# Attention kernel: chunk 0 in two query halves, reciprocals spread by TensorE from 16 columns, squares of the queries on VectorE

## The chip, the cores and the metric

The kernel runs on one core of a Trainium2 chip. The metric is the device time of one launch in microseconds (us). Most executions of one kernel agree within 0.3%; faster or slower is given at 2%. The profiled spans are 1.8 to 2.0 us shorter than the times of the same runs.

## The reference, cut to what matters

```python
x = A_x                                    # 1 x 2048 x 448, bf16
xn = _layernorm(x)
q, k, v = split(xn @ wqkv)                 # 16 heads of 28
p = softmax(q @ k.T * 28 ** -0.5)          # 16 x 2048 x 2048
s = merge(p @ v) @ wo
g = silu(gelu(xn @ w1 + b1) @ w2 + b2)     # 448 -> 1792 -> 448
return x + s * g
```

Dominant are the exponentials: 16 x 2048 x 2048 = 67 million.

## The kernel before

The Python file is a planner. Generators hand out tasks with an engine, an estimated duration and a priority; a list scheduler orders them and writes one program per engine, each strictly in order, with semaphores between them. **Whatever changes a duration or a task can change the order of everything after it.**

The work is cut into 16 blocks (4 groups of 4 heads, 4 chunks of 512 queries). A block has 64 score tiles of 128 keys x 512 queries. TensorE writes scores to a ring of PSUM banks, ScalarE takes exponentials of two (block 0) or three tiles at a time, TensorE multiplies them with v into `acc`. In some units the third tile is given to VectorE, which computes its exponential with a polynomial ("late" tiles, mostly in pairs of 1024 columns):

```python
def pick_late(self, u):            # is the third tile of unit u given to VectorE?
    ...
    left = (n - 1 - r) / 3.0 * 1.364 + LATE_SLACK      # time left in the block; LATE_SLACK = 6.0
    ...
        bl = K.backlog()                               # VectorE work that is waiting
        if not K.ys or bl > LATE_TH or bl + 4.8 > left or sub > LATE_SUB:   # LATE_TH = 8.0
            return False
```

The queries of a block are projected, squared on GpSimd, and get a norm term that TensorE sums:

```python
def p_q(self, g, c):
    ...
    yield _Task(DVE, lambda eng: eng.tensor_copy(qb, bank), [tok], [qr], 0.7, 0.0, 2)
    ...
    yield _Task(POOL, lambda eng: eng.tensor_tensor(qs, qb, qb, ALU.mult), [qr], [tq], 1.05, 0.0, 0)
    ...   # TensorE: bsel x qs, then VectorE adds it to qb
```

At a block's end the sums of the softmax become 128 x 16 reciprocals. GpSimd spreads each of the 16 columns over 32 and splits it in two bf16 parts; TensorE turns them round with an identity matrix:

```python
def p_epi(self, b):
    ...
    yield _Task(DVE, lambda eng: eng.reciprocal(K.rc[:, :], bank[:, 0:16]), ...)
    rcb = K.rc[:, :, None].to_broadcast([128, 16, 32])
    yield _Task(POOL, lambda eng: eng.tensor_copy(K.rhi[:, :, :], rcb), ...)
    yield _Task(POOL, lambda eng: eng.tensor_tensor(K.rlo[:, :, :], rcb, K.rhi[:, :, :], ALU.subtract), ...)
    ...
            for q in range(4):
                for k, r in enumerate((K.rhi, K.rlo)):
                    ap = r[:, 4 * q:4 * q + 4, :].rearrange("p a b -> p (a b)")
                    ins = eng.matmul(bank2[:, 128 * q:128 * (q + 1)], ap, K.ident[:, :], ...)
```

The dummy matmuls of zeros that appear in the trace (output `acc`, inputs `ident` and `zero`) are put in where the planner finds TensorE's recent use low, so that its clock stays up.

The softmax here doesn't subtract the row's maximum and nothing guards it: scores larger than these inputs give would overflow.

Of the kernel before, what the change touches and what calls it, by code (L numbers as in the profile page):

```python
# [16 lines left out]
DH = 28  # L17
# [27 lines left out]
for _m in sorted(MLATE):  # L45
    UOF[_m] = UOF[_m - 1]
LATE_GAP, LATE_TH, LATE_SLACK, LATE_SUB = 3, 8.0, 6.0, 14
NU = len(UNITS)
# [4 lines left out]
KNORM = 2.5  # L53
PV_START = 8
HAM_WIN, HAM_LOW, DUM = 3.4, 0.85, 0.17
# [37 lines left out]
class _Kernel:  # L93
# [167 lines left out]
    def alloc(self):  # L261
# [35 lines left out]
        self.rc = sb("rc", [128, 16], f32)  # L297
        self.rhi = sb("rhi", [128, 16, 32], bf)
        self.rlo = sb("rlo", [128, 16, 32], bf)
        self.zero = sb("zero", [128, 128], bf)  # L300
# [41 lines left out]
        self.b_x0h, self.b_vpad0 = [B(), B()], B()  # L342
        self.b_x0 = [B(), B()]
        self.b_kT = [[B() for _ in range(C)] for _ in range(G)]
        self.b_qT = [[B() for _ in range(C)] for _ in range(G)]
# [130 lines left out]
    def constants(self):  # L476
# [18 lines left out]
        def late_pads():  # L495
            yield ("until", lambda: K.b_xnT[0][1].tw is not None)

            def f(eng):
                eng.memset(K.wv[64:128, 3, :], 0.0)
                eng.memset(K.wv[0:64, 3, D:WS], 0.0)  # L500
                return eng.memset(K.wv[:, 0:3, D:WS], 0.0)
            yield _Task(DVE, f, [], [K.b_wvpad], 0.4, 0.05, 1)
            yield ("until", lambda: K.ln_done == 2 * C)
            yield _Task(DVE, lambda eng: eng.memset(K.w1[64:128, 3, :], 0.0), [], [K.b_w1pad], 0.8, 0.05, 4)
            K.dma(SP, lambda eng: eng.dma_start(K.w1[64:65, 3, :], K.B_b1.rearrange("(o f) -> o f", o=1)), K.s_b1,
                  writes=[K.b_w1pad], land=K.now + 4)
# [45 lines left out]
        def vpads():  # L552
            yield ("until", lambda: K.ready(K.b_xn[0], -0.1))
            yield _Task(POOL, lambda eng: eng.memset(K.vaug[:, :, :, DH:DH + 1], 2.0), K.b_xn[0], [K.b_vpad0], 1.2, 0.05, 2)
            yield _Task(POOL, lambda eng: eng.memset(K.vaug[:, :, :, DH + 1:32], 0.0), [K.b_vpad0], [K.b_vpad], 1.2, 0.05, 2)
# [4 lines left out]
    def loads(self):  # L560
# [11 lines left out]
        def lw(n0, n1, sem, tok, land):  # L572
            for k in range(KT):
                rows = slice(128 * k, min(128 * k + 128, D))
                ld(sv[0:rows.stop - rows.start, k, :, n0:n1], wqk[rows, :, n0:n1], sem, [tok] if k == KT - 1 else [], land)
        lw(0, 4 * DH, K.s_w["wqk"], K.b_stg, 6.5)
        ld(K.x_sb[:, 1, :, :], xr[1], K.s_x[1], [K.b_x[1]], 8.0)
# [28 lines left out]
    def p_ln(self, c):  # L606
# [5 lines left out]
        for h, ts in enumerate(hs):  # L612
            for t in ts:
                i = 4 * c + t
                yield _Task(DVE, lambda eng, i=i, t=t: eng.bn_stats(K.st6[:, i, :], K.x_sb[:, c, t, :]),  # L615
                            [K.b_x0[h] if c == 0 else K.b_x[c]], [K.b_st[c][h]], 0.61, 0.05, prio)

            def f(eng, ts=ts):
                ins = None
                for i in range(4 * c + ts[0], 4 * c + ts[-1] + 1):  # L620
                    ins = eng.bn_aggr(K.mv[:, i, :], K.st6[:, i, :])
                return ins
            yield _Task(DVE, f, [K.b_st[c][h]], [K.b_mv[c][h]], 0.1 * len(ts), 0.05, prio)
            K.spawn(K.p_ln2(c, h, ts), c)

    def p_ln2(self, c, h, ts):
# [11 lines left out]
        for t in ts:  # L638
            i = 4 * c + t
            rd = [K.b_x0[h] if c == 0 else K.b_x[c], K.b_mv[c][h], K.b_rs[c][h], K.b_pads]  # L640
            if c == 0:
                yield _Task(DVE, lambda eng, i=i, t=t: eng.tensor_scalar(
# [50 lines left out]

    def relayout(self, E, which, g0, g1, dur):
        K = self
        src = K.stg[:, :, which, 4 * g0:4 * g1, :]
        dst = (K.wq, K.wk)[which][:, :, 128 * g0:128 * g1].rearrange("p k (h e) -> p k h e", e=32)[:, :, :, 0:DH]
        if E == ACT:
# [15 lines left out]
    def p_first(self):  # L714
# [3 lines left out]
        def weights():  # L718
            yield ("until", lambda: K.b_rs[0][1].tw is not None)
            yield K.relayout(ACT, 0, 0, 1, 0.56)  # L720
            yield K.relayout(ACT, 1, 0, 1, 0.56)
            yield K.wsquare(ACT, 0, 1, 0.56)
            K.stg_done += 1
# [21 lines left out]
        def tr(pr, h):  # L745
# [3 lines left out]
            def f(eng):  # L749
# [5 lines left out]
                return ins  # L755
            return _Task(PE, f, K.b_xn[0][2 * h:2 * h + 2] + [K.b_id], [tok], 0.45, 0.2, 0)

        def trev(pr):
            for h in range(2):
                bank, tok = ring(4 * h + pr)  # L760
                src = bank.bitcast(dt.bfloat16)[:, 0:512].rearrange("p (k n) -> p k n", k=2)
                dst = K.xnT[:, 2 * pr:2 * pr + 2, 256 * h:256 * h + 256]
                rd = [tok] + ([K.b_x0h[pr]] if h else [])
                wr = [K.b_xnT[0][pr] if h else K.b_x0h[pr]]
                if pr == 0:
                    yield _Task(ACT, lambda eng, dst=dst, src=src: eng.activation(dst, src, ACTF.Copy), rd, wr, 0.6, 0.0, 0)
                else:
                    yield _Task(DVE, lambda eng, dst=dst, src=src: eng.tensor_copy(dst, src), rd, wr, 0.42, 0.0, 0)
        for h in range(2):
            for pr in range(2):  # L770
                yield tr(pr, h)
                if h == 0:
                    K.spawn(trev(pr), 0)
        K.spawn(K.p_k0(), 1)
        qps, qtok = ring(0)
        for k in range(2):
            yield K.t_proj(0, 0, 0, qps, qtok, k, 0)
        yield _Task(ACT, lambda eng: eng.activation(K.qsq[:, 0, :], qps, ACTF.Square), [qtok], [K.b_qsq[0]], 0.6, 0.0, 0)

        def f(eng):  # L780
            return eng.matmul(qps, K.bsel[:, :], K.qsq[:, 0, :], start=False, stop=True, skip_group_check=True)
        yield _Task(PE, f, [K.b_qsq[0], K.b_bsel], [qtok], 0.22, 0.15, 0)
        yield _Task(DVE, lambda eng: eng.tensor_scalar(K.qT[:, 0, 0:512], qps, K.colK[:, 0:1], None, op0=ALU.add),
                    [qtok, K.b_colK], [K.b_qT[0][0]], 0.75, 0.0, 0)

# [18 lines left out]
    def p_busy(self):  # L804
# [10 lines left out]
        while K.exp_u < NU - 2:  # L815
# [3 lines left out]
            if n > 2000:  # L819
                raise RuntimeError("stuck")  # L820

    def p_k0(self):
        K = self
        bank, tok = K.ring[:, 1, :], K.b_ring[1]
        for k in range(2):
            yield K.t_proj(1, 0, 0, bank, tok, k, 1)
        yield K.t_kev(ACT, 0, 0, bank, tok, 1)

# [50 lines left out]
    def p_q(self, g, c):  # L879
# [10 lines left out]
        qs, tq = K.qsq[:, i, :], K.b_qsq[i]  # L890
        yield _Task(POOL, lambda eng: eng.tensor_tensor(qs, qb, qb, ALU.mult), [qr], [tq], 1.05, 0.0, 0)  # L891
        bank2, tok2 = yield ("bank", lambda: K.ready([tq]) and (g == 0 or K.norms_done))
# [171 lines left out]
    def p_scores(self):  # L1064
        K = self
        for u in range(NU):
# [3 lines left out]
            for k in range(4):  # L1070
                for m, b, j, pc, _, _ in ps:
# [10 lines left out]
                    fl.append(f)  # L1082
                    rd += [K.b_qT[g][c], K.b_kT[g][t // 4]]

# [15 lines left out]
    def p_exps(self):  # L1100
        K = self
        for u in range(NU):
# [5 lines left out]
            def fexp(eng, b0=b0, p0=p0, n=n):  # L1108
                return eng.activation(K.P[:, p0:p0 + n, :], K.ring[:, b0:b0 + n, :], ACTF.Exp, scale=SM_SCALE)  # L1109
            yield _Task(ACT, fexp, [K.b_ring[b0 + k] for k in range(n)], [K.b_P[p0 + k] for k in range(n)],  # L1110
                        0.0843 + 0.4267 * n, 0.08, 3)
            for m in ms:
# [46 lines left out]
    def pick_late(self, u):  # L1159
# [8 lines left out]
        if len(ms) < 3 or not K.late_on or sub == 0 or r < 4 or GU - 1 <= u <= GU + 1:  # L1168
            return False
        left = (n - 1 - r) / 3.0 * 1.364 + LATE_SLACK  # L1170
        if K.open:
# [9 lines left out]
        else:  # L1181
            bl = K.backlog()
            one = max(bl, 4.1) + 7.2 > left
            if not K.ys or bl > LATE_TH or bl + 4.8 > left or sub > LATE_SUB:
                return False
# [44 lines left out]
    def p_exp2(self, ms, i):  # L1230
# [8 lines left out]
        tv, tu, ty = K.b_ev[n], K.b_eu[n], K.b_y[i][:len(ms)]  # L1239
        d0, d1 = (0.44, 0.74) if len(ms) == 1 else (0.71, 1.27)  # L1240
        if n == 1 and tv.w is None:
            for c in range(C):
                tv.r += K.b_kT[0][c].r
                tu.r += K.b_kT[1][c].r
# [95 lines left out]
    def p_epi(self, b):  # L1340
# [8 lines left out]
        def f(eng):  # L1349
            ins = None  # L1350
            for q in range(4):
# [4 lines left out]
        K.banks.append((bank, tok))  # L1356
        rcb = K.rc[:, :, None].to_broadcast([128, 16, 32])
        En, d1, d2 = POOL, 0.62, 1.05
        yield _Task(En, lambda eng: eng.tensor_copy(K.rhi[:, :, :], rcb), [K.b_rc], [K.b_rhl], d1, 0.0, 1)  # L1359
        yield _Task(En, lambda eng: eng.tensor_tensor(K.rlo[:, :, :], rcb, K.rhi[:, :, :], ALU.subtract),  # L1360
                    [K.b_rc, K.b_rhl], [K.b_rhl], d2, 0.0, 1)
        bank2, tok2 = yield ("bank", lambda: K.ready([K.b_rhl], 0.2))

        def f(eng):
            ins = None
            for q in range(4):
                for k, r in enumerate((K.rhi, K.rlo)):
                    ap = r[:, 4 * q:4 * q + 4, :].rearrange("p a b -> p (a b)")
                    ins = eng.matmul(bank2[:, 128 * q:128 * (q + 1)], ap, K.ident[:, :], start=(k == 0), stop=(k == 1),
                                     skip_group_check=True)  # L1370
            return ins
        yield _Task(PE, f, [K.b_rhl, K.b_id], [tok2], 0.55, 0.15, 3)
        dst = K.qT[:, g, c * 512:(c + 1) * 512]
# [101 lines left out]
```

## Time and profile before

| what | before |
|---|---|
| time, median of 4 runs | 490.1 us (490.01 to 490.25) |
| profiled span, mean granted clock of TensorE | 488.5 us, 0.994 |
| first exponential of scores starts | 13.74 us |
| late tiles | 67 |
| GpSimd busy | 86.5 us |

What ScalarE waited for (columns: total us, times, longest), exponentials only:

```profile
ACT P L1109 <- PE ring L1078: 3.7, 5, 1.2
ACT P L1109 <- PE acc L1295: 0.3, 1, 0.3
```

Four microseconds of waits are listed. The view leaves out short ones, so I also counted start to start in the trace: an exponential of three tiles follows the one before it by 1.331 us at the median, one of two by 0.905; what a gap has beyond that (and beyond the 1.587 of each of four tanh instructions that lie between) I call **stall**. Before has 10.7 us of stall: 2.6 before 45 us (block 0) and 8.1 after it.

The groups by form that the change touches (busy us, mean ns of one):

```profile
L1360 POOL TENSOR_TENSOR rlo<-rc,rhi 128x512 bf16<-128x512 f32 x15 | 20.2, 1344 | 1.2
L891 POOL TENSOR_TENSOR qsq<-qT 128x512 bf16<-128x512 bf16 x15 | 23.7, 1581 | 122.6 <-DVE qT L886 100.8 <-PE acc L811 21.8
L1247 DVE SCALAR_TENSOR_TENSOR kT<-kT 128x1024 f32<-128x1024 f32 x17 | 21.3, 1254 | 0.1
```

The square averages 1,581 ns, but its fastest takes 1,039; the 124 VectorE operations of 1024 columns with two inputs (L1247 is one kind) average 1,263 ns; undisturbed they take about 1,215 (the median).

### The profile page before, as it was taken

How to read it: one execution, taken by the hardware profiler on the slowest of the kernel's cores; microseconds unless marked ns; L12 is line 12 of the kernel's file. 1: busy time of each engine (PE TensorE's matmuls, PEld its weight loads, DVE VectorE, ACT ScalarE, POOL GpSimd, SP SyncE). 2: the span in 40 equal slices, each digit the busy share in tenths (PEclk: the TensorE clock that was granted, in tenths of full speed). 3: DMA queues.
4: the chain of work that ended last, by engine and by line, in shares of the span. 5: the costliest groups of instructions: out<-in, count | busy, mean ns of one | idle time of the engine just before them, and what ended most of it. 6: DMA issues, size and time to landing. Idle time of an engine off the chain costs nothing.

```text
span 488.5 us, 9994 instructions
## 1 busy us (share of the span) xinstructions
PE 449.2 (92%) x4143; PEld 177.4 (36%) x4179; DVE 404.8 (83%) x580; ACT 470.7 (96%) x391; POOL 86.5 (18%) x91
## 2 busy tenths in 40 slices
PE   6999999998988898999999999999999999989995
PEld 4443334333332332333333343233333333433653
DVE  8744899889998999999998299998988979878454
ACT  4999999999999999999999999999999999999994
POOL 6472112023021212020101022220200102020100
PEclk9999999999999999999999999999999999999998
DMA  8401000000000000000400000000101010101010
GB/s 250 142 12 26 1 0 1 1 1 3 0 1 1 1 0 1 2 2 0 129 5 1 0 2 1 0 2 1 38 1 40 1 38 1 58 20 38 4 50 30
DMA packets 8287, 11.08 MB, mean 23 GB/s; under 512 B 1649, under 2 KB 6897, under 8 KB 8242
## 3 DMA queue, kind: packets, MB, share of 16 engines
q1 hardware_dynamic: 8098, 10.21, 6.9%
q8 instruction: 33, 0.54, 0.5%
q10 hardware_dynamic: 144, 0.23, 0.1%
q14 instruction: 12, 0.10, 0.1%
HBM read 8.61 MB, written 1.84 MB: 21 GB/s over the span
## 4 chain that ended last, share of the span: by engine, by line
PE 37%; ACT 29%; issue 18%; DVE 12%; POOL 2%; DMA 1%; ACTq 0%; DVEq 0%; POOLq 0%
ACT P L1109 24%; PE ring L1078 11%; PE acc L1295 7%; PE misc L1026 5%; PE acc L811 4%; ACT h L1005 3%; PE misc L968 3%; PE misc L680 2%; DVE x_sb L1253 2%; PE misc L1384 1%; POOL rlo L1360 1%; DVE x_sb L1132 1%; ACT w L1040 1%; DVE st L615 1%; DVE kT L1247 1%
## 5 line engine op out<-in xcount | busy, mean ns | idle before, releaser
L1109 ACT ACTIVATE P<-ring 128x1536 bf16<-128x1536 f32 (+1 forms) x350 | 430.1, 1427 | 4.8 <-PE ring L1078 3.7
L1078 PE MATMUL ring<-qT,kT 32*128 32x512 bf16 (+1 forms) x1208 | 136.5, 350 | 17.4 <-ACT P L1109 13.3
L1295 PE MATMUL acc<-P,vaug 128*32 128x512 bf16 (+1 forms) x1141 | 93.8, 351 | 2.1 <-DVE E_sb L1345 0.7
L1078 PEld LDWEIGHTS ring<-qT,kT 32*128 32x128 bf16 x1208 | 36.6, 91 | 124.8 <-ACT P L1109 109.7
L1359 POOL CAST rhi<-rc 128x512 bf16<-128x512 f32 x15 | 19.5, 1297 | 239.7 <-DVE rc L1355 198.3
L811 PE MATMUL acc<-ident,zero 128*128 128x128 bf16 x660 | 56.4, 221 | 1.1 <-POOL qsq L891 0.6
L1132 DVE TENSOR_SCALAR x_sb<-ring 128x512 int32<-128x512 f32 x67 | 45.9, 686 | 10.4 <-PE ring L1078 9.5
L1026 PE MATMUL misc<-w,h 128*128 128x448 bf16 x224 | 51.9, 355 | 0.3
L811 PEld LDWEIGHTS acc<-ident,zero 128*128 128x128 bf16 x660 | 38.6, 98 | 24.5 <-issue 20.5
L891 POOL TENSOR_TENSOR qsq<-qT 128x512 bf16<-128x512 bf16 x15 | 23.7, 1581 | 122.6 <-DVE qT L886 100.8
L1295 PEld LDWEIGHTS acc<-P,vaug 128*32 128x32 bf16 x1141 | 24.5, 94 | 49.6 <-issue 42.3
L968 PE MATMUL misc<-xnT,w 128*128 128x512 bf16 x127 | 36.7, 382 | 2.0 <-issue 1.5
L951 DVE CAST h<-misc 128x512 bf16<-128x512 f32 x35 | 24.0, 687 | 5.4 <-PE misc L968 5.2
L1026 PEld LDWEIGHTS misc<-w,h 128*128 128x128 bf16 x224 | 17.4, 97 | 24.0 <-issue 10.6
L1251 DVE SCALAR_TENSOR_TENSOR kT<-kT 128x1024 f32<-128x1024 f32 (+1 forms) x23 | 25.8, 1121 | 0.3
L1253 DVE SCALAR_TENSOR_TENSOR x_sb<-x_sb,kT 128x1024 uint16<-128x1024 int32 (+1 forms) x23 | 25.5, 1110 | 0.3
L1247 DVE SCALAR_TENSOR_TENSOR kT<-kT 128x1024 f32<-128x1024 f32 (+1 forms) x23 | 25.5, 1107 | 0.3
L1249 DVE SCALAR_TENSOR_TENSOR kT<-kT 128x1024 f32<-128x1024 f32 (+1 forms) x23 | 25.1, 1092 | 0.3
L1251 DVE SCALAR_TENSOR_TENSOR w<-w 128x1024 f32<-128x1024 f32 (+1 forms) x21 | 23.2, 1105 | 0.2
L1247 DVE SCALAR_TENSOR_TENSOR w<-w 128x1024 f32<-128x1024 f32 (+1 forms) x21 | 22.7, 1079 | 0.3
L1249 DVE SCALAR_TENSOR_TENSOR w<-w 128x1024 f32<-128x1024 f32 (+1 forms) x21 | 22.7, 1082 | 0.1
L1253 DVE SCALAR_TENSOR_TENSOR x_sb<-x_sb,w 128x1024 uint16<-128x1024 int32 (+1 forms) x21 | 22.5, 1073 | 0.2
(144 smaller groups left out, 471.3 us busy)
## 6 DMA issues: line engine op xcount, KB each, us to landing
h<-in_A_x_dram SPq DMA_DIRECT2D x4, 448.0 KB, 3.3
w<-in_B_w_dram SPq DMA_DIRECT2D x1, 1568.0 KB, 7.3
x_sb<-in_A_x_dram SPq DMA_DIRECT2D x3, 448.0 KB, 5.2
w<-in_B_w_dram SPq DMA_DIRECT2D x1, 1344.0 KB, 9.0
out_dram<-h SPq DMA_DIRECT2D x6, 224.0 KB, 1.9
h<-in_A_wqkv_dram SPq DMA_DIRECT2D x3, 168.0 KB, 5.4
out_dram<-h SPq DMA_DIRECT2D x4, 112.0 KB, 1.7
wo<-in_A_wo_dram SPq DMA_DIRECT2D x16, 24.5 KB
```

The source lines that it names most:

```text
L811: ins = eng.matmul(K.acc[:, 0:128], K.zero[:, :], K.ident[:, :], start=False, stop=True, skip_group_check=True)
L951: yield _Task(DVE, lambda eng: eng.tensor_copy(dst, bank), [tok], wr, 0.69, 0.0, 2)
L968: ins = eng.matmul(bank, K.w1[:, kt, ft * 128:(ft + 1) * 128], K.xnT[:, kt, c * 512:(c + 1) * 512], start=(kt == 0), stop=(kt == KT - 1))
L1026: ins = eng.matmul(ps, hv[:, ft, t * 128:(t + 1) * 128], K.w2[:, ft, :], start=(ft == 0), stop=(ft == FT - 1))
L1078: return eng.matmul(K.ring[:, RB[m], col:col + nq], K.kT[32 * j:32 * j + 32, g, t * 128:(t + 1) * 128], K.qT[32 * j:32 * j + 32, g, c * 51 ...
L1109: return eng.activation(K.P[:, p0:p0 + n, :], K.ring[:, b0:b0 + n, :], ACTF.Exp, scale=SM_SCALE)
L1132: yield _Task(DVE, lambda eng, m=m, i=i, half=half: eng.tensor_scalar(K.ysb[i][:, 512 * half:512 * half + 512], K.ring[:, RB[m], :], SM_SC ...
L1247: yield _Task(DVE, lambda eng: eng.scalar_tensor_tensor(u, v, EXP_A, v, op0=ALU.add, op1=ALU.mult), [tv], [tu], d1, 0.0, 4)
L1249: yield _Task(DVE, lambda eng: eng.scalar_tensor_tensor(u, u, EXP_B, u, op0=ALU.add, op1=ALU.mult), [tu], [tu], d1, 0.0, 4)
L1251: yield _Task(DVE, lambda eng: eng.scalar_tensor_tensor(u, v, EXP_D, u, op0=ALU.mult, op1=ALU.add), [tv, tu], [tu], d1, 0.0, 4)
L1253: yield _Task(DVE, lambda eng: eng.scalar_tensor_tensor(pl.bitcast(dt.uint16), y, 2.0 ** -9, u, op0=ALU.mult, op1=ALU.add), ty + [tu], [K. ...
L1295: return eng.matmul(K.acc[32 * j:32 * j + 32, q0:q0 + nq], K.vaug[:, t, 4 * g + j, :], ap[:, col:col + nq], tile_position=(0, 32 * j), sta ...
```

## The change

It has four intents: start the exponentials earlier (chunk 0's queries in two halves of 256, so that their transposes, projections and norms overlap), unload GpSimd (reciprocals as 16 columns, spread by 32 narrow matmuls; squares of the queries and half of the layer norms on VectorE), and set the lateness limits anew for each block. Core of the diff, the start cut to its essence:

```diff
-LATE_GAP, LATE_TH, LATE_SLACK, LATE_SUB = 3, 8.0, 6.0, 14
+LATE_GAP, LATE_SUB = 3, 14
+THS = (8.0, 4.0, 7.0, 6.0, 4.0, 6.0, 9.0, 6.0, 3.0, 3.0, 8.0, 8.0, 8.0, 3.0, 6.0, 8.0)
+SLACKS = (6.0, 5.0, 6.5, 5.0, 9.0, 6.5, 9.0, 6.0, 3.0, 4.0, 6.0, 6.0, 8.0, 6.0, 8.0, 6.0)
-PV_START = 8
+PV_START = 5
...
-            if c == 0:
+            if c == 0 or t % 2 == 0:          # layer norm of these rows on VectorE, the others on GpSimd
...
+    def p_q0(self, h, bank, tok):             # for each half h of chunk 0's queries
+        ps, c0 = bank[:, 0:256], 256 * h
+        yield _Task(ACT, ... eng.activation(K.qsq[:, 0, c0:c0 + 256], ps, ACTF.Square) ...)
+        yield _Task(PE, ... eng.matmul(ps, K.bsel[:, :], K.qsq[:, 0, c0:c0 + 256], ...) ...)
+        yield _Task(DVE, ... eng.tensor_scalar(K.qT[:, 0, c0:c0 + 256], ps, K.colK[:, 0:1], None, op0=ALU.add) ...)
...
-        yield _Task(POOL, lambda eng: eng.tensor_tensor(qs, qb, qb, ALU.mult), [qr], [tq], 1.05, 0.0, 0)
+        yield _Task(DVE, lambda eng: eng.tensor_tensor(qs, qb, qb, ALU.mult), [qr], [tq], 0.43, 0.0, 2)
...
-                        0.0843 + 0.4267 * n, 0.08, 3)      # planner's duration of an exponential
+                        0.0725 + 0.4267 * n, 0.08, 3)
...
-        yield _Task(En, lambda eng: eng.tensor_copy(K.rhi[:, :, :], rcb), ...)
-        yield _Task(En, lambda eng: eng.tensor_tensor(K.rlo[:, :, :], rcb, K.rhi[:, :, :], ALU.subtract), ...)
+        yield _Task(POOL, lambda eng: eng.tensor_copy(K.rhi[:, :], K.rc[:, :]), ...)
+        yield _Task(POOL, lambda eng: eng.tensor_tensor(K.rlo[:, :], K.rc[:, :], K.rhi[:, :], ALU.subtract), ...)
...
-                    ins = eng.matmul(bank2[:, 128 * q:128 * (q + 1)], ap, K.ident[:, :], ...)
+                    for j in range(4):
+                        ins = eng.matmul(bank2[32 * j:32 * j + 32, 128 * q:128 * (q + 1)],
+                                         r[:, 4 * q + j:4 * q + j + 1].to_broadcast([128, 32]), K.ident[:, :],
+                                         tile_position=(0, 32 * j), ...)
```

## The prediction

> **What bounds the kernel now.** I read the page first: busy shares, then the 40 slices.
>
> ```profile
> PE 449.2 (92%) x4143; PEld 177.4 (36%) x4179; DVE 404.8 (83%) x580; ACT 470.7 (96%) x391; POOL 86.5 (18%) x91
> ...
> ACT  4999999999999999999999999999999999999994
> ```
>
> ScalarE (ACT) is the bound: it has work in all slices but the first and the last. TensorE's 92% is padded: 56.4 us of it are 660 matmuls of zeros (row L811 of the groups) that only keep its clock up. So the time is: when the first exponential of scores starts, plus ScalarE's work, plus ScalarE's waits, plus the tail after the last exponential. Only what shortens one of these four counts.
>
> **The start**, from the timeline:
>
> ```profile
> 12.52 0.73 DVE L783 TENSOR_SCALAR qT<-ring,colK 128x512 bf16<-128x512 f32 x1
> ...
> 13.31 0.39 PE L1078 MATMUL ring<-qT,kT 32*128 32x512 bf16 x4
> ...
> 13.74 6.57 ACT L1109 ACTIVATE P<-ring 128x1024 bf16<-128x1024 f32 x7 [0.39 <-PE ring L1078]
> ```
>
> The first exponential starts at 13.74 us. Ahead of it stands a serial chain on all 512 queries of chunk 0: evacuation of the transposes, projection (10.19 to 11.31), square (11.35 to 11.95), the norm's matmul (12.04 to 12.42), eviction (12.52 to 13.25), scores.
>
> **The work.** Groups by form: 250 exponentials of three 512-column tiles, 99 of two. Start to start I measured medians of 1,331 and 905 ns in the trace. 67 of the 99 are units that gave their third tile to VectorE ("late" tiles, row L1132, x67), so one more late tile saves ScalarE 0.43 us. It costs VectorE some 3.6 us: 0.69 for the eviction, and half of 0.71 + 4 x 1.26 for a pair.
>
> **The waits.** Of ScalarE's waits between 40 and 482 us, three are long. One is in the timeline at 155, two at 437:
>
> ```profile
> 154.66 1.42 POOL L891 TENSOR_TENSOR qsq<-qT 128x512 bf16<-128x512 bf16 x1 [16.70 <-PE acc L811]
> ...
> 155.22 1.41 DVE L1253 SCALAR_TENSOR_TENSOR x_sb<-x_sb,w 128x512 uint16<-128x512 int32 x1
> ...
> 156.68 0.40 PE L1295 MATMUL acc<-P,vaug 128*32 128x512 bf16 x4 [0.57 <-DVE x_sb L1253]
> ...
> 157.88 2.37 ACT L1109 ACTIVATE P<-ring 128x1536 bf16<-128x1536 f32 x2 [0.55 <-PE ring L1078]
> ```
>
> ```profile
> 433.07 1.50 POOL L1359 CAST rhi<-rc 128x512 bf16<-128x512 f32 x1 [22.23 <-DVE rc L1355]
> ...
> 434.65 2.09 POOL L1360 TENSOR_TENSOR rlo<-rc,rhi 128x512 bf16<-128x512 f32 x1
> ...
> 436.79 0.23 PE L1369 MATMUL misc<-ident,rhi 128*128 128x128 bf16 x1 [1.65 <-POOL rlo L1360]
> ...
> 437.78 2.79 ACT L1109 ACTIVATE P<-ring 128x1536 bf16<-128x1536 f32 x2 [1.15 <-PE ring L1078]
> ...
> 441.44 2.42 ACT L1109 ACTIVATE P<-ring 128x1536 bf16<-128x1536 f32 x2 [0.87 <-PE ring L1078]
> ```
>
> The reader is to see one pattern. In the first, L1253 on 512 columns takes 1.41 us instead of its 0.69, beside GpSimd's (POOL's) square. TensorE's in-order stream waits for it, and scores queued behind come late: ScalarE idles 0.55. In the second, GpSimd's spread of the reciprocals takes 1.50 + 2.09 us where the last block's takes 0.61 + 1.05; TensorE waits 1.65 for it ahead of the next scores, and ScalarE loses 1.15. TensorE's clock then drops (granted 0.95 in 420 to 440; four L1384 matmuls take 1.70 us instead of 0.93), which costs another 0.87. Sum 2.57 us.
>
> **What the Trainium skill says.** "SBUF — State Buffer", section "Who interferes with whom": a VectorE instruction with two SBUF inputs contends with a GpSimd instruction that reads SBUF. The trace agrees: L1251 at 65.71 takes 1.64 instead of 1.22 us beside a square that takes 1.95 instead of 1.04. "TensorE: Matmul & The Clock Gate", Part 1: idleness lowers TensorE's clock; the stretch at 437 to 441 agrees. The same page, Part 3: 32-column tiles run side by side, measured 2.38 times for three. The trace agrees: 32 context matmuls of 128 columns, four abreast, take 0.63 us at 474.02. "VectorE: DVE Perf Modes", the perf-mode tier table: a 16-bit tensor_tensor in SBUF runs at two elements a cycle. The trace has 0.39 us for 448 columns (L1395); for 512 I estimate 0.42.
>
> **The change, part by part.**
>
> Start. Three pieces. (a) The weights of q are laid out in ScalarE's idle time between 6.07 and 7.17; the weights' fourth transfer is issued at 2.66 and takes 3.8, so lands near 6.5, just in time. The squares of the weights (0.58) leave ScalarE. It therefore takes the second half's transposes at about 9.1, not 9.46: xnT is complete near 9.85 instead of 10.24, saving 0.4. (b) The last half's square, norm matmul and eviction work on 256 columns. I estimate 0.37, 0.24 and 0.46 against 0.60, 0.38 and 0.73: saves 0.6. (c) Four matmuls of 256 columns replace four of 512 that ran with a norm matmul between (1.12 us, to some 0.65): saves 0.4. Against that, the first half's square, norm matmul, evictions and key projection share the queues: give back 0.3. Net 1.1: first exponential near 12.65.
>
> Reciprocals. Per block, 15 times, GpSimd's 1.30 + 1.34 us (rows L1359, L1360; 39.7 us in all) become two operations on 16 columns, near 0.2 each like L523's 0.19. TensorE's eight matmuls (0.62 at 436.79) become 32 narrow ones, four abreast: 0.63 by the comparison above. TensorE loses nothing; the wait for GpSimd shrinks by 2 to 3 us a block, which only counted at 437: 1.15 + 0.87 = 2.02 us.
>
> Squares. 15 of 1.58 us leave GpSimd (23.7), and 15 x 0.42 = 6.3 us come to VectorE. Six normalisations (0.38) go to VectorE too: 2.3. Against this, VectorE's two-input operations are no longer stretched: 124 of 1024 columns average 1.26 against 1.22 undisturbed, 5 us. VectorE is thus about 3 us worse. The wait at 157 (0.55) goes.
>
> GpSimd: 86.5 - 39.7 - 23.7 - 4.3 + 30 x 0.2 + 1 = near 26 us.
>
> Thresholds. Ten of them are lowered and a few slacks raised, VectorE's times in the planner are shortened (1.27 to 1.14). I can't derive the number of late tiles from that. VectorE idles 7.6 us in 360 to 400 and 10.5 in 420 to 460, but under 2 in most stretches of 20 us before 260. I choose three more late tiles, 70 instead of 67: 3 x 0.43 = 1.3 us.
>
> Tail: from the last exponential's end (482.2) to the end 6.3 us; unchanged.
>
> Sum: -1.1 (start) - 2.6 (waits) - 1.3 (late tiles) + 1.0 (my allowance for small waits that a re-planned order brings; the present ones near block ends are 0.2 to 0.45 each) = -4.0. **486.0 us.**
>
> **Rivals.**
>
> (1) VectorE becomes the limit. The squares queue there, lower thresholds refuse late tiles. For it: it is 90% busy before 260 us. Against: the contention goes. Five late tiles fewer cost 2.1 us, so the time would be 489.5.
>
> (2) The early start is lost at once. The keys of chunk 2 are late already:
>
> ```profile
> 28.92 0.75 DVE L691 TENSOR_SCALAR kT<-ring,ecol 128x512 bf16<-128x512 f32 x1 [2.19 <-PE ring L680]
> ...
> 30.16 6.78 ACT L1109 ACTIVATE P<-ring 128x1024 bf16<-128x1024 f32 x7 [0.75 <-PE ring L1078]
> ```
>
> An exponential that arrives 1.1 earlier waits 1.1 longer, unless the keys come earlier too. They should: with half of the normalisations on VectorE, GpSimd's 2.81 us for chunk 2 become 1.4. If they don't, 487.1.
>
> (3) Weight loads that read one column 32 times are slow. 32 one after another at the 95 ns of a load would be 3 us, in order ahead of the scores: 1 to 1.5 us of ScalarE idle per block, 15 to 22 us in all, time over 500. Nothing in this trace shows such a load; the narrow ones here (row L1295) overlap. Small chance.
>
> (4) Everything goes well and VectorE's idle time in the second half fills with eight late tiles: -1.1 - 2.6 - 3.4 = 483.
>
> **Range and chances.** From (4) and (1), trimmed: 483.2 to 488.6. Faster by over 2% means under 480.2, which needs some fourteen more late tiles on top of all else: 4%. Slower by over 2% needs (3): 2%. Within 2%: 94%.
>
> **What the changed profile would show.** First exponential at 12.4 to 12.9. The gap at 30 gone or under 0.9. No ScalarE wait over 0.5 us after 40 us, and TensorE's clock never down before the tail. GpSimd near 26 us, its two spread operations under 0.3 us each; the 32 spread matmuls within 0.7 us. VectorE's 1024-column operations at 1.21 to 1.23 on average, its busy time 405 to 425. Two-tile exponentials: 96 to 110 instead of 99. Wrong would make me: fewer late tiles, spread matmuls over 1 us, or new waits at each block's end.

## The result, and the profile after

| | before | after |
|---|---|---|
| time, median of 4 runs | 490.1 us (490.01 to 490.25) | 486.96 us (486.47 to 488.1) |
| profiled span, granted clock | 488.5, 0.994 | 484.7, 0.997 |
| first exponential | 13.74 | 12.61 |
| late tiles | 67 | 62 |
| stall in block 0 / after 45 us | 2.57 / 8.15 | 2.17 / 3.54 |
| VectorE two-input operations of 1024 columns, mean | 1,263 ns (x124) | 1,219 ns (x132) |

The ratio is 0.9939 (95%: 0.9921 to 0.9957), so "same" by the 2% rule, though the interval excludes 1. (Ratios are the mean time of one kernel's runs over that of the other's of the same rounds, so not quite the ratio of the medians quoted.) The profiled pair differs by 3.8 us of span, a little more than the medians' 3.1, because the profiled run of the changed kernel was the fastest of its four, and that of the kernel before (490.38) was above its four.

The head of the page, as it answers to the first fence of the prediction:

```profile
PE 438.8 (91%) x4393; PEld 170.2 (35%) x4428; DVE 389.7 (80%) x562; ACT 471.8 (97%) x393; POOL 34.5 (7%) x71
...
ACT  5999999999999999999999999999999999999994
```

GpSimd went from 86.5 to 34.5 us, VectorE from 404.8 to 389.7 although it took over work: it has fewer late tiles, and its operations are no longer stretched. ScalarE is still the bound in every slice. The start, from the timeline:

```profile
11.64 0.48 DVE L814 TENSOR_SCALAR qT<-ring,colK 128x256 bf16<-128x256 f32 x1
...
12.61 1.02 ACT L1136 ACTIVATE P<-ring 128x1024 bf16<-128x1024 f32 x1 [0.42 <-PE ring L1105]
```

The eviction of the second half of the queries takes 0.48 us where all 512 took 0.73, and ends at 12.12 instead of 13.25. ScalarE's waits for exponentials, and the groups that were changed:

```profile
ACT P L1136 <- PE ring L1105: 0.4, 1, 0.4
```

```profile
L1384 POOL CAST rhi<-rc 128x16 bf16<-128x16 f32 x15 | 7.8, 521 | 403.7 <-DVE rc L1382 304.4 <-PE acc L1322 73.8 <-PE ring L1105 25.5
L1385 POOL TENSOR_TENSOR rlo<-rc,rhi 128x16 bf16<-128x16 f32 x15 | 6.2, 413 | 1.2
L918 DVE TENSOR_TENSOR qsq<-qT 128x512 bf16<-128x512 bf16 x15 | 6.3, 419 | 0.4
L1274 DVE SCALAR_TENSOR_TENSOR kT<-kT 128x1024 f32<-128x1024 f32 x18 | 21.9, 1216 | 0.3
L1136 ACT ACTIVATE P<-ring 128x1024 bf16<-128x1024 f32 x94 | 101.9, 1126 | 0.7 <-PE ring L1105 0.4
```

The one wait left in the first view is that of the first exponential itself. In the second, the spread takes 521 and 413 ns on GpSimd, more than the 200 I expected; the VectorE operation L1274 is back at its undisturbed 1,216 ns; and of the 94 two-tile exponentials 32 belong to block 0, which leaves 62 late tiles. Last, the stretch from 420 to 460 us in the view by windows (columns: length, then busy us and count of PE, PEld, DVE, ACT, POOL, then clock, DMA share, GB/s), first before, then after:

```profile
420.00:460.00 40.00, 36.18 (x449) 16.74 (x447) 29.45 (x45) 37.86 (x31) 4.85 (x4) 0.96 0.09 34
```

```profile
420.00:460.00 40.00, 35.92 (x554) 17.43 (x555) 27.34 (x40) 40.00 (x32) 2.24 (x4) 1.00 0.05 19
```

ScalarE was idle for 2.1 of these 40 us and is not any more; the clock of TensorE no longer drops.

**Where the 3.8 us of span come from.** First exponential 1.13 earlier; stall in block 0 down 0.40; stall after 45 us down 4.61, of which the three long waits that the prediction shows are 3.24 counted start to start; five late tiles fewer put 5 x 0.43 = 2.13 us of exponentials back on ScalarE; tail 0.10 shorter; the rest, some 0.3, lies in the gelu stretch (0.13 longer) and the last exponentials. -1.13 - 0.40 - 4.61 + 2.13 - 0.10 + 0.3 = -3.8.

### The profile page after: what moved, and what is told of

It is laid out like the page before. It is cut to its first block, busy times and chain, and to the rows that moved or that the text cites. A ratio compares the mean times of both kernels' runs of the same rounds, so it can differ in the third digit from the quotient of the medians.

```text
span 484.7 us, 10440 instructions
## 1 busy us (share of the span) xinstructions
PE 438.8 (91%) x4393; PEld 170.2 (35%) x4428; DVE 389.7 (80%) x562; ACT 471.8 (97%) x393; POOL 34.5 (7%) x71
## 4 chain that ended last, share of the span: by engine, by line
ACT 45%; PE 34%; issue 16%; DVE 3%; POOL 0%; ACTq 0%; DVEq 0%
ACT P L1136 43%; PE ring L1105 9%; PE acc L1322 5%; PE misc L1053 5%; PE ring L995 4%; PE acc L845 2%; PE misc L683 2%; PE misc L995 1%; PE misc L1411 1%; PE acc L827 1%; ACT h L1032 1%; ACT w L1067 1%; PE ring L937 1%; PE misc L1394 0%; PE misc L1246 0%
## 5 line engine op out<-in xcount | busy, mean ns | idle before, releaser
L1322 PE MATMUL acc<-P,vaug 128*32 128x512 bf16 (+1 forms) x1146 | 94.8, 351 | 1.2 <-DVE E_sb L1372 0.5
L1159 DVE TENSOR_SCALAR x_sb<-ring 128x512 int32<-128x512 f32 x62 | 42.6, 688 | 20.8 <-PE ring L1105 20.2
L845 PE MATMUL acc<-ident,zero 128*128 128x128 bf16 x546 | 47.0, 221 | 0.6 <-DVE E_sb L1372 0.4
L1322 PEld LDWEIGHTS acc<-P,vaug 128*32 128x32 bf16 x1146 | 25.1, 94 | 49.9 <-issue 45.0
L845 PEld LDWEIGHTS acc<-ident,zero 128*128 128x128 bf16 x546 | 31.6, 98 | 20.7 <-issue 16.9
L995 PE MATMUL misc<-xnT,w 128*128 128x512 bf16 x125 | 35.2, 382 | 1.9 <-issue 1.4
L1384 POOL CAST rhi<-rc 128x16 bf16<-128x16 f32 x15 | 7.8, 521 | 403.7 <-DVE rc L1382 304.4
L1276 DVE SCALAR_TENSOR_TENSOR kT<-kT 128x1024 f32<-128x1024 f32 (+1 forms) x20 | 23.3, 1167 | 0.3
L1278 DVE SCALAR_TENSOR_TENSOR kT<-kT 128x1024 f32<-128x1024 f32 (+1 forms) x20 | 23.3, 1167 | 0.3
L1280 DVE SCALAR_TENSOR_TENSOR x_sb<-x_sb,kT 128x1024 uint16<-128x1024 int32 (+1 forms) x20 | 23.3, 1164 | 0.4
L1274 DVE SCALAR_TENSOR_TENSOR kT<-kT 128x1024 f32<-128x1024 f32 (+1 forms) x20 | 23.3, 1163 | 0.4
L995 PE MATMUL ring<-xnT,w 128*128 128x512 bf16 x81 | 19.5, 380 | 0.9 <-ACT h L1032 0.7
L1274 DVE SCALAR_TENSOR_TENSOR w<-w 128x1024 f32<-128x1024 f32 (+1 forms) x17 | 19.7, 1159 | 0.3
L1278 DVE SCALAR_TENSOR_TENSOR w<-w 128x1024 f32<-128x1024 f32 (+1 forms) x17 | 19.7, 1157 | 0.3
L1280 DVE SCALAR_TENSOR_TENSOR x_sb<-x_sb,w 128x1024 uint16<-128x1024 int32 (+1 forms) x17 | 19.7, 1156 | 0.2
L1276 DVE SCALAR_TENSOR_TENSOR w<-w 128x1024 f32<-128x1024 f32 (+1 forms) x17 | 19.6, 1154 | 0.1
```

Of the source, the lines that this page charges most:

```text
L845: ins = eng.matmul(K.acc[:, 0:128], K.zero[:, :], K.ident[:, :], start=False, stop=True, skip_group_check=True)
L995: ins = eng.matmul(bank, K.w1[:, kt, ft * 128:(ft + 1) * 128], K.xnT[:, kt, c * 512:(c + 1) * 512], start=(kt == 0), stop=(kt == KT - 1))
L1159: yield _Task(DVE, lambda eng, m=m, i=i, half=half: eng.tensor_scalar(K.ysb[i][:, 512 * half:512 * half + 512], K.ring[:, RB[m], :], SM_SC ...
L1274: yield _Task(DVE, lambda eng: eng.scalar_tensor_tensor(u, v, EXP_A, v, op0=ALU.add, op1=ALU.mult), [tv], [tu], d1, 0.0, 4)
L1276: yield _Task(DVE, lambda eng: eng.scalar_tensor_tensor(u, u, EXP_B, u, op0=ALU.add, op1=ALU.mult), [tu], [tu], d1, 0.0, 4)
L1278: yield _Task(DVE, lambda eng: eng.scalar_tensor_tensor(u, v, EXP_D, u, op0=ALU.mult, op1=ALU.add), [tv, tu], [tu], d1, 0.0, 4)
```

## The experiments

Names beginning with b are the kernel before with one part of the change; those beginning with a are the changed kernel with one part undone or altered. They ran in three batches, beside which the kernel before had medians of 490.03, 490.06 and 489.93. "Stall" is counted as above, after 45 us.

| run | median us | ratio (95%) | late | first exp. | stall after 45 us |
|---|---|---|---|---|---|
| before | 490.1 | | 67 | 13.74 | 8.15 |
| after | 486.96 | 0.9939 (0.9921-0.9957) | 62 | 12.61 | 3.54 |
| b_narrow | 487.37 | 0.9946 (0.9933-0.9958) | 67 | 13.98 | 5.01 |
| b_start | 486.82 | 0.9940 (0.9927-0.9952) | 67 | 12.81 | 5.80 |
| b_squares | 493.41 | 1.0068 (1.0055-1.0080) | 69 | 13.50 | 9.12 |
| a_noise | 491.99 | 1.0044 (1.0030-1.0058) | 62 | 13.17 | 8.02 |
| a_th4 | 489.98 | 1.0000 (0.9988-1.0011) | 54 | 12.68 | 3.21 |
| a_th9 | 490.40 | 1.0016 (1.0002-1.0030) | 71 | 12.65 | 10.66 |
| a_wide | 489.40 | 0.9983 (0.9970-0.9996) | 61 | 12.84 | 5.94 |
| a_poolsq | 488.01 | 0.9961 (0.9949-0.9974) | 61 | 12.68 | 4.04 |
| b_narrow_start | 486.73 | 0.9935 (0.9923-0.9947) | 67 | 12.97 | 4.66 |
| a_t1 | 486.93 | 0.9940 (0.9923-0.9957) | 68 | 12.54 | 5.14 |
| a_t4 | 484.76 | 0.9908 (0.9893-0.9923) | 67 | 12.84 | 3.35 |
| a_poolxn | 490.48 | 1.0028 (1.0002-1.0055) | 59 | 12.43 | 2.92 |

The first exponential of one and the same start varies by half a microsecond and more from run to run (13.50 to 13.98 with the old one, 12.43 to 13.17 with the new one), so differences of that size there mean nothing. The means are 13.74 (3 profiles) and 12.75 (11), so the new start gains about 1.0.

The runs also differ by TensorE's clock. In seven of the profiles (before, b_start, b_squares, a_noise, a_wide, a_poolsq and a_t1) the granted clock falls to half for one stretch of 3.4 us, in four of them after TensorE had idled for 0.7 to 1.7 us at a time. Before and a_noise by windows (the clock is the third number from the right):

```profile
438.14:441.56 3.42, 3.42 (x20) 1.09 (x18) 1.76 (x3) 2.55 (x3) 0.00 (x0) 0.50 0.00 0
```

```profile
108.45:111.86 3.41, 3.41 (x18) 0.62 (x18) 3.34 (x5) 2.08 (x3) 0.80 (x1) 0.50 0.00 0
```

Of the runs without a profile only the mean clock is on record. Of the 31 runs of before beside the experiments, ten have a mean of 0.996 or more and took 489.40 to 489.56 us; the others have 0.994 or less and took 489.78 to 490.59. The changed kernel's slowest run (488.1 us) has 0.994 against 0.997 to 0.999 in the other three. So some tenths of a microsecond in before, and 2 in two runs of a_t4, go with the clock of the single run. What makes it fall in one run and not in another was not tested.

### Narrow reciprocals alone, order held

```diff
-        self.rhi = sb("rhi", [128, 16, 32], bf)      # rlo likewise
+        self.rhi = sb("rhi", [128, 16], bf)
 # two GpSimd operations on 16 columns and 32 narrow matmuls as in the change,
 # but the planner keeps the old durations 0.62, 1.05 and 0.55: every engine keeps its order
```

> The kernel before with only the reciprocals changed to 16 columns and 32 narrow matmuls; the planner keeps the old durations, so that every engine has its old order. My theory (GpSimd's slow spread cost 1.15 + 0.87 us at 437 us and nothing elsewhere): 488.1 us, no ScalarE wait at 437, 67 late tiles. Rival (another wait takes its place, or narrow matmuls with repeated columns are slow): 490 us or more.

487.37 us, 2.66 less than before. As the order is the same instruction for instruction, this is the cleanest of all runs. ScalarE's waits:

```profile
ACT P L1109 <- PE ring L1078: 1.7, 3, 0.8
```

Two of the five waits are gone, those at 437 and 441 us in the prediction's fence: in the start-to-start count 1.36 and 0.98 us of stall vanish, 2.34 together. All stall after 45 us fell by 3.14, so 0.8 went elsewhere; "nothing elsewhere" in my theory was wrong. The 32 narrow matmuls took 0.62 us on TensorE (434.78 to 435.40), their weight loads 92 to 97 ns each and overlapping; so **rival 3 is dead**. The VectorE operations of 1024 columns fell from 1,263 to 1,225 ns. The gain was larger than the prediction's 2.02 for this part.

### The early start alone, old limits

```diff
+    # p_first, p_q0, the weights and their layout as in the change
 # left as before: reciprocals, squares, layer norms, LATE_TH and LATE_SLACK
```

> The kernel before with only chunk 0 in two halves (no normalisations moved to VectorE, old thresholds; planned again). My theory: first exponential near 12.6 us and 489.0 us. Rival (the keys of chunk 2 take it back): first exponential as early, but ScalarE waits 1.5 us or more for scores near 29 us, and the time is 490.0 us.

486.82 us, 3.2 less than before, and neither number I expected. The first exponential is 0.93 us earlier, and no stall appears at 28 us to take it back, although the layer norms stayed on GpSimd. The other 2 us come from elsewhere: even in its profile, stall after 265 us is 2.08 instead of 4.59. The waits at 437 and 441 are gone here as well, without any change to the reciprocals, because the planner laid out the rest differently. **A run that lets the planner re-plan tests the part and a new order together.** Only b_narrow and a_noise (and b_narrow_start against b_start) hold the order; the others are read with that in mind. And the profile of b_start fell on its slowest run (488.22 us, the other four 486.72 to 486.96): in it the clock fell to half at 44.23 us, and the 1.15 us of stall at 47.76 follow. Its stall in the table is thus too high for the other runs by about 1.3 us.

### Squares on VectorE alone, old limits

```diff
-        yield _Task(POOL, lambda eng: eng.tensor_tensor(qs, qb, qb, ALU.mult), [qr], [tq], 1.05, 0.0, 0)
+        yield _Task(DVE, lambda eng: eng.tensor_tensor(qs, qb, qb, ALU.mult), [qr], [tq], 0.43, 0.0, 2)
```

> The kernel before with only the squares of the queries on VectorE (old thresholds; planned again, 69 late tiles instead of 67). My theory (less contention, late tiles worth 0.43 us each): 490.1 - 0.55 - 0.85 = 488.7 us. Rival (without new thresholds VectorE is overbooked, so scores and context matmuls wait for it): 491 us or more, with ScalarE waits over 0.5 us at block ends.

493.41 us, 3.4 more than before. The waits:

```profile
ACT P L1109 <- PE acc L1295: 3.2, 3, 1.4
...
ACT h L1005 <- PE ring L968: 2.4, 1, 2.4
```

The kind that was 0.3 us is 3.2: at 133.45 and 135.79, at a block's end, exponentials wait for the context matmuls (L1295), which come behind VectorE's late tiles. These are waits as in rival 1, VectorE as the limit. But they are the smaller part: all stall after 45 us is only 0.97 us higher, and two more late tiles save 0.85. The gelu stretch, which stall leaves out, takes 30.65 us instead of 28.10, 2.42 of it in the one wait of the second line, at 275.96. Shortly before, TensorE had waited for GpSimd's wide spread (which ends at 269.71) and then for VectorE's L1374 (until 271.40). The order is a new one, so this run doesn't show how much of the 3.4 us the squares themselves cost.

### GpSimd's load put back as operations that nobody waits for

```diff
+    def noise(self, n):                     # on GpSimd, into a scratch buffer nobody reads
+        ... eng.tensor_tensor(self.scr, ident, ident, ALU.mult) ... # 128 x 512, bf16
 # noise(1) after each eviction of the queries, where the square was; noise(2) after rlo at each block's end
```

> The changed kernel with GpSimd's old load put back as operations that nobody waits for: one 512-column tensor_tensor beside each square, two after each spread. All other engines keep their order. Theory (waits for GpSimd in order cost, contention alone costs little): within 0.6 us of the changed kernel's 487.0, VectorE's 1024-column operations back at 1.25 us or more. Rival (contention itself is what cost): 488.5 to 489.5 us, with ScalarE waits back.

The order of all other engines is that of the changed kernel, GpSimd is busy for 91.3 us, a little more than the 86.5 before the change, and the results of its 45 added operations are not used. If the removed *wait* had been all, nothing should happen. It cost 5.0 us: 491.99, more than the rival's range too. Stall after 45 us went from 3.54 to 8.02. TensorE's listed waits for GpSimd are the same as without the added operations (1.0 and 0.7 us). One of the places, from the timeline:

```profile
103.83 2.48 POOL L1377 TENSOR_TENSOR scr<-ident 128x512 bf16<-128x512 bf16 x2
...
104.10 1.31 DVE L1277 TENSOR_SCALAR w<-x_sb 128x1024 f32<-128x1024 uint16 x1
105.45 1.94 DVE L1278 SCALAR_TENSOR_TENSOR w<-w 128x1024 f32<-128x1024 f32 x1
107.31 0.68 DVE L1414 TENSOR_TENSOR qT<-misc,E_sb 128x512 bf16<-128x512 f32 x1
...
108.05 0.68 PE L685 MATMUL misc<-xnT,wq 128*128 128x512 bf16 x2 [1.26 <-DVE qT L1414]
...
109.32 1.45 ACT L1140 ACTIVATE P<-ring 128x1536 bf16<-128x1536 f32 x1 [0.73 <-PE ring L1109]
```

The reader is to see a chain of four engines. Beside GpSimd's two scratch operations, which last until 106.31, VectorE takes 1.31 us for what takes 0.69 elsewhere, then 1.94 instead of 1.22. Its next operation, L1414, therefore ends late; TensorE, in order, waits 1.26 us for it ahead of the next scores; ScalarE waits 0.73. Nobody waits for GpSimd here. Then TensorE's clock falls to half from 108.45 to 111.86 us (the window shown above), and ScalarE stalls twice more, at 111.38 and 113.29. The three stalls come to 2.2 us, half of what the run added. All five runs have a mean clock of 0.989 to 0.994, the changed kernel's 0.994 to 0.999: a part of the price of contention is paid through the clock, it seems. VectorE's busy time rose from 389.7 to 402.4 us. My theory before this run, that the direct waits for GpSimd carry most of the gain and contention little, **fell**: contention alone, with the falls of the clock that it brings, is worth up to 5 us in this order (a bit less for the load that was really taken away, which was smaller).

### One limit for all blocks: 4 and 9

```diff
-THS = (8.0, 4.0, 7.0, 6.0, 4.0, 6.0, 9.0, 6.0, 3.0, 3.0, 8.0, 8.0, 8.0, 3.0, 6.0, 8.0)
-SLACKS = (6.0, 5.0, 6.5, 5.0, 9.0, 6.5, 9.0, 6.0, 3.0, 4.0, 6.0, 6.0, 8.0, 6.0, 8.0, 6.0)
+THS = (4.0,) * 16       # a_th4;  a_th9: (9.0,) * 16
+SLACKS = (6.0,) * 16
```

> The changed kernel with thresholds of 4 and slacks of 6: 54 late tiles instead of 62. My arithmetic: 487.0 + 8 x 0.43 = 490.4 us, stalls unchanged. Rival (fewer late tiles also take stalls away): 489 us or less, stalls after 45 us under 3 us.

> The changed kernel with thresholds of 9 and slacks of 6 in every block: 71 late tiles instead of 62, VectorE's backlog allowed to grow. My prediction's arithmetic (each late tile saves 0.43 us and costs nothing else): 487.0 - 9 x 0.43 = 483.1 us. Rival (an overbooked VectorE delays its evictions, TensorE waits in order and so does ScalarE): 487.5 us or more, ScalarE's stalls after 45 us 7 us or more instead of 3.5.

Late tiles 54 and 71, against 62. (With the old limits of 8 and 6 the planner stops with an error on the changed kernel, so some limit had to change. But it finishes with 6 and 6, 8 and 5 or 8 and 7 in all blocks, so a set block by block was not needed for that. These were only built, not run.) Fewer tiles: 489.98 us, 3.0 more than the changed kernel; 8 x 0.43 = 3.4 is what the tiles account for, and stall is about the same, 3.21. Up to here each late tile is worth its 0.43 us. More tiles: 490.40, also more by 3.4, although nine tiles should save 3.9. Stall went from 3.54 to 10.66:

```profile
ACT P L1136 <- PE acc L1322: 5.2, 4, 2.6
```

```profile
430.07 1.22 DVE L1280 SCALAR_TENSOR_TENSOR x_sb<-x_sb,kT 128x1024 uint16<-128x1024 int32 x1
...
431.75 0.60 PE L1322 MATMUL acc<-x_sb,vaug 128*32 128x512 bf16 x5
...
432.48 2.79 ACT L1136 ACTIVATE P<-ring 128x1536 bf16<-128x1536 f32 x2 [2.61 <-PE acc L1322]
```

At a block's end the last context matmuls (L1322, which read the late tiles' `x_sb`) cannot run before VectorE has finished the last late tile at 431.29, and the exponentials run out of buffers that these matmuls free: 2.61 us of ScalarE, six times what a late tile saves. So late tiles have a price on both sides, and what decides is not their number alone but where VectorE's queue stands at the end of each block.

### Wide reciprocals, and squares on GpSimd, in the changed kernel

```diff
 # a_wide: rhi, rlo, their two operations and the eight matmuls as before the change
 # a_poolsq:
-        yield _Task(DVE, lambda eng: eng.tensor_tensor(qs, qb, qb, ALU.mult), [qr], [tq], 0.43, 0.0, 2)
+        yield _Task(POOL, lambda eng: eng.tensor_tensor(qs, qb, qb, ALU.mult), [qr], [tq], 1.05, 0.0, 0)
```

> The changed kernel with the reciprocals spread by GpSimd to 512 columns again (planned again with those durations, 61 late tiles). Theory (GpSimd's long reads stretch VectorE and the spread stands in TensorE's way): 489 to 490 us, stalls after 45 us 5.5 us or more, VectorE's 1024-column operations near 1.25 us. Rival (the new plan makes room for it): 487.4 us, the one late tile's worth.

> The changed kernel with the queries' squares on GpSimd again (planned again, 61 late tiles). Theory (15 long reads of GpSimd beside VectorE's two-input operations cost ScalarE): 488.3 us or more, stalls after 45 us 4.3 us or more. Rival (only the reciprocals' contention counted): 487.4 us, the late tile's worth.

Undoing the reciprocals costs 2.4 us (489.40), of which 0.43 is one late tile fewer, and the old wait returns near the same place:

```profile
432.59 1.90 POOL L1387 TENSOR_TENSOR rlo<-rc,rhi 128x512 bf16<-128x512 f32 x1
...
435.55 2.79 ACT L1136 ACTIVATE P<-ring 128x1536 bf16<-128x1536 f32 x2 [0.96 <-PE ring L1105]
```

In three of its five runs the clock is 0.994, and in the profile 1.17 us of its stall, at 47.37, follow a fall of the clock at 44.65; the two runs at 0.996 and 0.997 took 488.65 and 488.61.

Undoing the squares costs 1.05 us (488.01), of which 0.43 is one late tile fewer; the stall of 4.04 lies, like the time, between the two expectations. So with the new limits the squares on VectorE seem to help a little, where b_squares, with the old ones, was 3.4 slower.

### Reciprocals and start together, old limits

```diff
 # b_start, and the reciprocals of b_narrow with the planner's old durations
```

> The kernel before with the start in halves and the narrow reciprocals, in the order of the run with the start alone (486.8 us): squares still on GpSimd, old thresholds, 67 late tiles. Theory (the re-planned order of that run already escaped the wait at 437 us, so the narrow reciprocals only take contention away): 485.8 us. Rival (the two gains add, -3.2 and -2.7): 484.1 us. In both cases the squares and thresholds of the change would not have been needed.

486.73 us: the gains of the two, 2.7 and 3.2, do not add up; I had expected some 0.9 less. The order of b_start had already lost the waits that narrow reciprocals take away. And it equals the changed kernel (486.96) **without** squares on VectorE, layer norms on VectorE or new limits. These three together bought nothing that can be measured in this choice of limits. Even b_start alone, with the old reciprocals, takes 486.82: the start and the order that the planner then found give, as far as can be measured, all that the whole change gives.

### All later layer norms on GpSimd again

```diff
-            if c == 0 or t % 2 == 0:
+            if c == 0:
```

> The changed kernel with the normalisations of chunks 1 to 3 on GpSimd alone again (planned again, 59 late tiles). My prediction's rival 2 (the keys of chunk 2 then come late): a ScalarE stall of 0.8 us or more near 28 us, and 487.0 + 3 x 0.43 + 0.9 = 489.2 us. Other theory (the keys are in time anyway, as in the run with the start alone): no stall there over 0.5 us, 488.3 us.

490.48 us, 3.5 more (one run of six, 494.84, had a granted clock of 0.984; the others are 489.89 to 491.8). Rival 2 had placed the danger at 28 us. Both expectations (489.2 and 488.3) are missed. There is one stall of 3.17 us, but at 22 to 26:

```profile
25.88 1.94 ACT L1136 ACTIVATE P<-ring 128x1024 bf16<-128x1024 f32 x2 [2.47 <-PE acc L1322]
```

The exponential waits for context matmuls, so for room in the P buffers, not for keys. The planner ordered the rest anew (59 late tiles), so this run doesn't show that half of the layer norms *must* be on VectorE.

### Two other sets of limits

```diff
+THS = (8.0, 7.0, 8.0, 6.0, 6.0, 7.0, 5.0, 9.0, 9.0, 9.0, 7.0, 9.0, 10.0, 7.0, 8.0, 8.0)        # a_t4
+SLACKS = (6.0, 3.0, 5.0, 8.0, 3.0, 5.5, 6.0, 6.0, 7.0, 6.0, 9.0, 10.0, 10.0, 7.0, 5.0, 6.0)
-                        0.0725 + 0.4267 * n, 0.08, 3)
+                        0.051 + 0.4267 * n, 0.08, 3)
 # a_t1: another set of THS and SLACKS, the duration left at 0.0725
```

> The changed kernel with other thresholds and slacks, block by block, for which the planner finds 68 late tiles without waits of its own making. If six more late tiles come without new stalls: 487.0 - 6 x 0.43 = 484.4 us, stalls 5.7 us. Rival (as with 71 late tiles, an overbooked VectorE gives it back): 487 us or more, stalls 8 us or more.

> As the last one, with 67 late tiles, and with the planner's cost of an exponential lowered to 1.331 us for three tiles, the start-to-start time in the traces. Without new stalls 484.9 us; rival: 487 us or more, because the plan's slack is gone.

a_t1 has 68 late tiles and 486.93 us: its six more tiles save 2.6, its stall after 45 us is 1.6 higher, and its runs spread from 485.47 to 488.25; the expectation is missed. (By spans it is some 1.1 us faster than the changed kernel, 484.0 against 485.15 at the median; four of its six times are 2.5 to 3.1 us above their spans, and why is not known.) **a_t4 is the fastest: 484.76 us**, as expected (484.9), ratio 0.9908, 5.2 less than the kernel before. By medians it is 2.2 less than the changed kernel, by the ratios 1.5, and the two intervals just touch. Two of its six runs took 486.48, with a clock of 0.991 instead of 0.997 to 0.999. It has 67 late tiles as before the change, and no more stall than the changed kernel (3.35):

```profile
PE 433.9 (90%) x4279; PEld 164.1 (34%) x4314; DVE 405.4 (84%) x587; ACT 469.5 (97%) x393; POOL 42.8 (9%) x71
```

VectorE is again as busy as before the change, 405.4 us, with the same number of late tiles, though it has squares and layer norms besides. The room for them is for the most part what the missing contention left: 124 operations that take some 1.21 us instead of 1.263 are 6 us. The rest comes from the polynomials' other operations, and from pairing: 34 pairs of late tiles and 7 single ones instead of 31 and 13. Five late tiles more than the changed kernel are 5 x 0.43 = 2.1 us, which is about the difference. Which of its two edits does it, the limits or the planner's duration of an exponential, was not tried apart.

## Why the prediction was right or wrong

486.0 was predicted, 486.96 measured, inside the range. But the sum is closer than its terms.

**Start (-1.1): right in sum, by luck in its parts.** 12.65 predicted, 12.61 measured, closer than one start repeats. Piece (a) failed. ScalarE does evacuate its last transposes early (until 9.80 us), but the last copy is VectorE's, and that ends at 10.33 us where it ended at 10.24 before:

```profile
9.83 0.41 DVE L768 COPY xnT<-ring 128x512 bf16<-128x512 bf16 x1
```

```profile
9.92 0.41 DVE L771 COPY xnT<-ring 128x512 bf16<-128x512 bf16 x1
```

So -0.4 became +0.1. From there the last projection ends after 0.51 us instead of 1.07 (0.56 saved, 0.4 predicted), the scores start 1.34 after that instead of 2.00 (0.66 saved, 0.6 predicted), and the 0.3 given back did not show. The gap at 30 us is gone. Block 0 lost 0.40 us of stall beyond that.

**Waits (-2.6, and +1.0 for new small ones): right in kind, too small.** The three long waits went, as predicted, by the mechanism that b_narrow shows with the order held: there 2.34 us of the 3.14 of stall that vanish are the two waits near 437. The clock that the prediction read as 0.95 over 20 us is half for 3.42 us, from 438.14. But all stall after 45 us fell by 4.61, where 2.6 - 1.0 = 1.6 was predicted. The allowance for new waits was wrong in sign: the small waits shrank as well. What I left out is the contention itself. I counted 5 us less of VectorE time and set them off against the squares and norms that VectorE takes over ("VectorE is thus about 3 us worse"; the sum gives 3.6), as if only the balance of busy time counted. a_noise shows that they count by where they fall: they delay operations that an in-order TensorE waits for, and put back into the same order they cost 5.0 us of time.

**Late tiles (-1.3): the step that failed.** "I choose three more late tiles, 70 instead of 67: 3 x 0.43 = 1.3 us." There were five fewer, +2.1 us: the lower limits refuse them, as the first half of rival 1 said; a_th9 and a_t1, which differ from the changed kernel in the limits alone, have 71 and 68. The price of 0.43 us held, as a_th4 shows; the number could not be had from busy shares. The direction could have been: ten limits go down, and a limit refuses tiles. (The prediction says that a few slacks are raised; six are, but four are lowered, which refuses tiles too.) I let VectorE's idle time after 360 us decide instead, but a_th9 shows that filling it costs more at the blocks' ends than it saves.

The two errors, 3.4 us for the tiles (+2.1 instead of -1.3) and 3.4 for the stalls (-5.0 in all instead of -1.6), cancel, and that the sum came so close is luck. They are not independent: a_th9 shows how stalls grow when tiles are added without regard to the blocks' ends.

**Rivals.** (1) came half true: its five fewer tiles, but not its time of 489.5, because the waits went with them; b_squares shows some of its waits, but most of its +3.4 lies in the gelu stretch. (2) did not come at 28 us in any run with the early start, with the norms on VectorE or not. (3) is dead, 0.62 us for 32 matmuls. (4) took the tiles from VectorE's idle time; a_t4 comes nearest to its 483 with 67.

**The checks.** VectorE's 1024-column operations: 1.219 us, as said; its squares 0.42 us, as estimated. No ScalarE wait over 0.5 us after 40 us, TensorE's clock not down before the tail: as said, in the profiled run (in the slowest of the four the mean clock was 0.994). Two-tile exponentials 94 (96 to 110 said) and VectorE's busy time 389.7 (405 to 425): wrong, both from the late tiles. GpSimd 34.5 instead of near 26, and its spread operations 521 and 413 ns instead of under 300: wrong. Of the 8.5 us, 14.0 - 6.0 = 8.0 are these two operations, and the trace shows why:

```profile
429.61 0.62 POOL L1384 CAST rhi<-rc 128x16 bf16<-128x16 f32 x1 [26.61 <-DVE rc L1382]
...
430.21 1.23 DVE L1274 SCALAR_TENSOR_TENSOR kT<-kT 128x1024 f32<-128x1024 f32 x1
...
430.31 1.20 POOL L1385 TENSOR_TENSOR rlo<-rc,rhi 128x16 bf16<-128x16 f32 x1
```

Alone, rlo takes 0.22 us (its fastest and its median). Here it starts 0.10 after L1274 and ends with it, 1.20 us later. It is blocked by an operation that came first, for as long as that lasts (the last section has what the skill says of this). **A shorter instruction blocks the other engine for less time, but is itself blocked as long as before.** That is why VectorE recovered its 1.22 us and GpSimd did not get down to 0.2.

**What stays open.** How much PV_START (8 to 5) and the planner's new durations contribute; what in the order of b_start avoids the waits at 437; why the gelu stretch of b_squares is longer; which edit makes a_t4.

## What to carry to other kernels

Read contention between two engines by where it falls, not by its sum: a few tenths of a microsecond on an operation that an in-order engine waits for reach the engine that bounds the kernel. When a planner lays out the program, hold the order fixed to test one part, or test it in more than one order; undoing one part of a change otherwise measures a new order too. After freeing an auxiliary engine, tune the amount of work that it takes over from the bound engine again: here that was worth some 2 us, where single parts of the change gave 2.7 (b_narrow) and 3.2 (b_start, with its new order). Contention's sum alone says little: in b_start VectorE's operations of 1024 columns average 1,286 ns, more than the 1,263 before, and it is 3.2 us faster.

## What the Trainium skill lacked or had wrong

- The Trainium skill, "SBUF — State Buffer", section "Who interferes with whom", has whoever issues first keep the shared ports for its whole instruction, and the other fully blocked. Nothing wrong: the trace agrees in both directions (rlo on 16 columns took 1.20 us instead of 0.22 behind a VectorE operation; a VectorE operation of 1.22 us took 1.94 behind a GpSimd one that had started before it). It lacks what follows for sizes. In b_narrow, with the order held, a GpSimd operand 32 times narrower brought VectorE's operations from 1,263 to 1,225 ns, but GpSimd's two operations still averaged 882 and 392 ns, against 196 and 214 for the fastest.
- The Trainium skill, "TensorE: Matmul & The Clock Gate", section "LDWEIGHTS (loading the stationary operand)", gives P / 1.2 ns for P columns, by estimate 27 ns for 32 and 107 for 128. The recorded weight loads of 32 columns took 92 to 97 ns, those of 128 columns mostly 95 to 99. (The profile models the ends of matmuls; whether those of loads are measured, no run shows, so the formula may still hold for the array.) It has no word on a load that reads one column 32 times: here such loads took the same 92 to 97 ns, and 32 of them with their matmuls, four abreast, 0.62 us.
- No page gives the fixed cost of a short GpSimd operation: the fastest on 128 x 16 took 196 ns (cast) and 215 ns (subtract) in the changed kernel. Spans on GpSimd are rough in this profile.
- No page says how to price contention in a program of in-order engines: 45 unused GpSimd operations (57.5 us) lengthened VectorE's busy time by 12.7 us and the kernel by 5.0.
